# Loads one buffer further ahead, stores on ScalarE's queue, and half of the value scaling on ScalarE, in a fused mLSTM, MoE and MLP kernel

## The chip, the core and the metric

The kernel runs on one core of one Trainium2 chip. The metric is the device time of one execution in microseconds; three runs of the kernel before gave 841.56, 841.85 and 846.75 us, median 841.85.

## The reference, cut to what matters

Three stages in a row, all float32. Only the first, the recurrent attention, is touched by the change.

```
def _attn_ref(q, k, v, i_gate, f_gate, o_gate):      # 4 batches, 8 heads, 768 tokens, 40 dims
    for t in range(S):
        m_new = max(f_gate[t] + m, i_gate[t])
        f_stab = exp(f_gate[t] + m - m_new);  i_stab = exp(i_gate[t] - m_new)
        C = f_stab * C + i_stab * outer(v[t], k[t])   # 40 x 40 state of each head
        n = f_stab * n + i_stab * k[t]
        y[t] = sigmoid(o_gate[t]) * (C @ q[t]) / max(abs(n . q[t]), 1)
x = y as 3072 tokens x 320
x = _moe_ref(x)     # greedy routing of tokens to 8 experts, 384 each; relu(x @ w1) @ w2
return _moe2_ref(x) # elu(x @ w_in) @ w_out
```

## The kernel before, in words

**Chunks and units.** The 768 tokens are cut into 12 chunks of 64. A unit `u` is one chunk `n = u // 2` of one pair of batches `bp = u % 2`, both batches side by side on the 128 partitions, so there are 24 units. `Attention.run` (from L456) has one pass, here called step `u`, for each unit. Inside a chunk the recurrence is written as small matrix products: scores (q times k), values (the decayed scores P times the scaled values `vp`), recall (the faded query `qt` times the state C) and state (`kt` times `vp`, into `pC`). The steps are pipelined: step `u` runs the values, recall and state of unit `u`, the scores of unit `w = u + 2`, and prepares unit `v = u + 1`.

**What each engine does in a step, in the order of its queue.**
- TensorE (PE): values of `u` with scores of `w` (L368, L283), recall and state (L382, L394), three transposes of the rows `x` of unit `u - 1` (`turn`, L438), three logits matmuls on them (`logits`, L448), and the decay rows of `w` (`decay`, L291, into `pF` and `pD`).
- VectorE (DVE): the scan W and the weighted scores P of unit `v` (L309, L359), the reciprocal of the denominator `rd` (L414, L416, L418), the new state (L405), the rows `x` (L427).
- GpSimd (POOL): `vp` (all eight heads' values times the input gate, L316), `qt` (L319), the output gate `sg` (L420), `kt` (L328), the faded state C (L330).
- ScalarE (ACT): the copy `xT` of the transposes (L440), the sigmoid `sg` (L354), the logits copy `L` (L449), the copy `db` of the decays (L302), a copy inside `x` (L429).
- SyncE (SP): the DMA issues. At the end of step `u` it stores the two halves of `x` to DRAM (L432; the last two units' stores are on ScalarE's queue), and at the end of every even step it loads `qk` and `vk` of chunk `u // 2 + 2` (L254, L258).

Beside this, from step 4 on, ten pieces of the MLP's first weight, which arrive as 64-bit numbers, are loaded (`cx`, L856) and turned into float32 (DVE L873, L877, L880; ACT `cg` L868 and `wih` L926; POOL `wil` L928), and parts of the router run ahead (`early`, DVE L608 to L628). `fl` in `run` places these pieces at fixed points of the step by the tables FP and EP. Every engine executes its queue in the order in which the program issues it.

**Buffers.** `qk`, `vk` and `vp` have two buffers each. A load of chunk `n + 2` goes into the buffer of chunk `n`, which is last read by `qt` and `kt` of unit `2n + 1` in step `2n`. The chunk is first needed by the scores that run in step `2n + 2`.

After step 23 the router's rounds, the experts and the MLP follow, ordered by a planner with times of its own; the change does not touch them.

Of the kernel before, what the change touches and what calls it, by code (L numbers as in the profile page):

```python
# [8 lines left out]
F32 = mybir.dt.float32  # L9
# [3 lines left out]
AF = mybir.ActivationFunctionType  # L13
ALU = mybir.AluOpType
# [3 lines left out]
NS, NU = 12, 24  # L18
# [16 lines left out]
class Plan:  # L35
# [46 lines left out]
    def next(self):  # L82
        self.due(min(self.todo)[0])
# [30 lines left out]
class Attention:  # L114
# [4 lines left out]
    def __init__(self, nc, tc, consts, qk, vk, ig, fg, wg, xd, L, ident):  # L119
        self.nc, self.tc, self.qk, self.vk, self.xd, self.L, self.ident = nc, tc, qk, vk, xd, L, ident  # L120
        self.es = ExitStack()
        one = self.es.enter_context(tc.tile_pool(name="a1", bufs=1))
        self.two = self.es.enter_context(tc.tile_pool(name="a2", bufs=2))
        self.psX = self.es.enter_context(tc.tile_pool(name="psX", bufs=1, space=PS))
        V, G, A = nc.vector, nc.gpsimd, nc.scalar
# [16 lines left out]
        warm = one.tile([1, 8], F32, name="warm")  # L142
        V.memset(warm, 0.0)
        A.activation(warm, warm, AF.Exp)
        self.QKb = [one.tile([128, 2, 2, 8, 64], F32, name=f"qk{i}") for i in range(2)]
        self.QK, self.VK, self.W = {}, {}, {}
        for bp in range(2):
            self.load_qk(0, bp)
# [2 lines left out]
        self.wg = one.tile([128, 3, 8], F32, name="wg")  # L151
        nc.sync.dma_start(self.wg, wg)
        self.load_vk(1)
        self.VP = [one.tile([128, 8, 64], F32, name=f"vp{i}") for i in range(2)]
        m = one.tile([32, S + 1], F32, name="m")
        V.memset(m[:, 0:1], -1e30)
        d1 = one.tile([32, S], F32, name="d1")
# [92 lines left out]
        self.nc.scalar.activation(self.isT[:, n0:n1].rearrange("p n h -> p (n h)"), self.pG[:, n0 * 16:n1 * 16], AF.Copy)  # L250

    def load_qk(self, n, bp=slice(0, 2)):
        self.QK[n] = self.QKb[n % 2]
        self.nc.sync.dma_start(self.QK[n][:, bp], self.qk[n, :, bp])  # L254

    def load_vk(self, n):
        self.VK[n] = self.two.tile([128, 2, 968], F32, name="vk")
        self.nc.sync.dma_start(self.VK[n], self.vk[n])  # L258

    def by_token(self, u, i):  # L260
# [51 lines left out]
    def factors(self, u):  # L312
        G = self.nc.gpsimd
        n, bp = divmod(u, 2)
        i_ = self.isT[:, n, bp * 8:bp * 8 + 8, None].to_broadcast([128, 8, 41])
        G.tensor_tensor(self.VP[u % 2][:, :, :41], self.by_token(u, 0), i_, op=ALU.mult)  # L316
        if n > 0:
            qt = self.st["q", u] = self.two.tile([128, 8, 64], F32, name="qt")
            G.tensor_tensor(qt, self.QK[n][:, bp, 1], self.st["D", u], op=ALU.mult)  # L319
# [41 lines left out]
    def values(self, u):  # L361

        n, bp = divmod(u, 2)
        o = self.st["O", u] = self.psum("pO", 2)
        P = self.st.pop(("P", u))

        def one(h, r):
            self.nc.tensor.matmul(o[64 - r:128 - r, h], P[r:r + 64, h], self.VP[u % 2][r:r + 64, h], start=h == 0,  # L368
                                  stop=n == 0 and h == 7)

        return one
# [15 lines left out]
    def state(self, u):  # L387
        n, bp = divmod(u, 2)
        if n == NS - 1:
            return None  # L390
        kt = self.st.pop(("k", u))

        def one(h, r):
            self.nc.tensor.matmul(self.pC[r:r + 40, h], kt[r:r + 64, h], self.VP[u % 2][r:r + 64, h], start=True, stop=True)  # L394

        return one

# [24 lines left out]
    def rows_out(self, u):  # L422

        nc = self.nc
        n, bp = divmod(u, 2)
        x = self.st["x", u] = self.two.tile([128, 384], F32, name="x", bufs=3)
        nc.vector.tensor_tensor(x[:, :320].rearrange("p (h d) -> p h d", d=40), self.st.pop(("O", u))[:, :, :40],  # L427
                                self.st.pop(("sg", u)), op=ALU.mult)
        nc.scalar.activation(x[:, 320:], x[:, 256:320], AF.Copy)  # L429
        for r in range(2):  # L430
            row = (bp * 2 + 1 - r) * S + n * 64
            (nc.scalar if u > NU - 3 else nc.sync).dma_start(self.xd[row:row + 64], x[r * 64:r * 64 + 64])  # L432

    def turn(self, u):
        x = self.st.pop(("x", u))
# [20 lines left out]
    def run(self, hook, fill):  # L456
        later = self.later()
        for u in range(NU):
            v, w = u + 1, u + 2
            fl = lambda i: ([fill() for _ in range(FP[i])] if u > FU else []) + [self.step() for _ in range(EP[i])]  # L460
            self.both(self.values(u), self.scores(w))
            self.both(self.recall(u), self.state(u))
            if u > 0:
                self.turn(u - 1)
            if v < NU:
                self.scan(v)
                self.factors(v)
                self.opens(v)
                self.weigh(v)
            fl(0)  # L470
            if u < 3:
                next(later, None)
            self.gates(u, fl)
            if v < NU:
                self.fade(v)
            if u > 0:
                self.logits(u - 1)
            fl(2)
            if w < NU:
                self.decay(w)  # L480
            self.add_state(u)
            fl(3)
            if u == NU - 1:
                while self.extra:
                    self.step()
            self.rows_out(u)
            fl(4)
            if u % 2 == 0 and u // 2 + 2 < NS:
                self.load_qk(u // 2 + 2)
                self.load_vk(u // 2 + 2)  # L490
            if u == 0:
                self.turn_gi(2, NS)
                self.keep_gi(2, NS)
            hook(u)
        self.turn(u)
        self.logits(u)
        hook(NU)
        self.es.close()
# [1011 lines left out]
```

## Time and profile before

| | us |
|---|---|
| median of three runs | 841.85 |
| the profiled execution | 841.95 |
| its span, first to last instruction | 840.2 |
| attention, to the last stores of x | 0 to 187 |
| router, experts and MLP | 187 to 840 |

The profiled execution is 0.1 us from the median; 1.75 us of it lie outside the span. The profile is read by stage, because a mean over the whole span hides that attention is a chain of 24 short steps over five engines while the rest is one long run of matmuls.

### The profile page before, as it was taken

The numbers are of one execution on the slowest core, as the hardware profiler recorded it, in microseconds if no ns is written. First come the engines' busy times: TensorE is split into PE (matmuls) and PEld (weight loads), VectorE is DVE, ScalarE is ACT, GpSimd is POOL, SyncE is SP. The second block draws the span as 40 slices with busy tenths as digits, with TensorE's granted clock in tenths as the row PEclk, the third lists the DMA queues.
The fourth block names the chain that finished last, engine by engine and source line by source line (L and its number), as shares of the span: only waits on it lengthen the run. The fifth ranks groups of instructions, "written<-read, shape, count | busy, mean of one in ns | idle before, by whom it ended". The sixth has DMA issues, their size and how long they took to land.

```text
span 840.2 us, 18328 instructions
## 1 busy us (share of the span) xinstructions
PE 730.2 (87%) x7355; PEld 679.3 (81%) x7355; DVE 584.1 (70%) x1616; ACT 349.7 (42%) x743; POOL 309.7 (37%) x358
## 2 busy tenths in 40 slices
PE   7776667682889979989999999999999999999995
PEld 5665656571778878878988988899999999999995
DVE  8773776858788996688788778966942862662452
ACT  5322333333526652454354435424633643542431
POOL 3665776743622651352422414410601411211001
PEclk9765988895699989989999999999999999999998
DMA  5565565623520410220310301300310220100000
GB/s 206 182 245 169 164 261 174 221 54 110 181 63 19 149 64 25 84 83 1 128 62 3 112 17 63 104 24 2 128 40 24 91 76 25 63 1 25 1 1 24
DMA packets 20757, 72.79 MB, mean 87 GB/s; under 512 B 3200, under 2 KB 7296, under 8 KB 19264
## 3 DMA queue, kind: packets, MB, share of 16 engines
q1 hardware_dynamic: 11856, 39.41, 13.8%
q0 software_dynamic: 8448, 31.73, 11.4%
q8 instruction: 58, 0.95, 0.5%
q10 hardware_dynamic: 368, 0.49, 0.2%
q14 instruction: 27, 0.22, 0.1%
HBM read 62.96 MB, written 8.65 MB: 85 GB/s over the span
## 4 chain that ended last, share of the span: by engine, by line
PE 52%; DVE 16%; issue 6%; ACT 3%; DMA 0%; POOL 0%; POOLq 0%; ACTq 0%; DVEq 0%
PE ph L1096 24%; PE acc L1234 5%; PE acc L1238 4%; PE acc L1235 4%; PE acc L1203 3%; PE acc L1205 2%; PE acc L1204 2%; DVE e L1149 2%; PE pr L727 2%; DVE gl L980 1%; PE acc L1190 1%; DVE ge L713 1%; PE acc L1192 1%; PE ph L1049 1%; ACT e L1146 1%
## 5 line engine op out<-in xcount | busy, mean ns | idle before, releaser
L1234 PE MATMUL acc<-woh,gh 128*128 128x320 f32 x384 | 123.1, 321 | 0.0
L1238 PE MATMUL acc<-woh,gl 128*128 128x320 f32 x384 | 120.0, 312 | 0.0
L1235 PE MATMUL acc<-wol,gh 128*128 128x320 f32 x384 | 119.4, 311 | 0.0
L1149 DVE SCALAR_TENSOR_TENSOR e<-e,ph 128x384 f32<-128x384 f32 x128 | 69.8, 549 | 61.9 <-ACT e L1146 61.5
L1145 ACT ACTIVATE e<-ph 128x384 f32<-128x384 f32 x128 | 62.6, 489 | 117.4 <-PE ph L1096 113.0
L980 POOL TENSOR_TENSOR gl<-e,gh 128x384 fp32r<-128x384 f32 x33 | 34.4, 1045 | 165.2 <-DVE gh L974 129.9
L1096 PE MATMUL ph<-yh,wih 128*128 128x384 f32 x256 | 90.2, 352 | 0.4
L1096 PE MATMUL ph<-yh,wil 128*128 128x384 f32 x256 | 86.6, 338 | 0.0
L1113 ACT ACTIVATE gh<-ph 128x384 fp32r<-128x384 f32 x64 | 31.3, 491 | 123.0 <-PE ph L1096 121.8
L1244 POOL DMA_INDIRECT out_dram<-ot,idx x24 | 24.0, 998 | 141.3 <-ACT ot L972 138.0
L1120 DVE SCALAR_TENSOR_TENSOR gl<-ph,gh 128x384 fp32r<-128x384 f32 x64 | 35.3, 554 | 56.3 <-ACT gh L1113 55.9
L1238 PEld LDWEIGHTS acc<-woh,gl 128*128 128x128 f32 x384 | 72.8, 190 | 0.6
L1234 PEld LDWEIGHTS acc<-woh,gh 128*128 128x128 f32 x384 | 73.0, 190 | 0.2
L1235 PEld LDWEIGHTS acc<-wol,gh 128*128 128x128 f32 x384 | 73.0, 190 | 0.0
L1146 ACT ACTIVATE e<-e 128x384 f32<-128x384 f32 x128 | 67.3, 526 | 4.0
L1096 PE MATMUL ph<-yl,wih 128*128 128x384 f32 x256 | 66.8, 342 | 0.0
L283 PE MATMUL pS<-qk 64*64 64x64 f32 x768 | 37.5, 268 | 29.5 <-DMA qk<-in_qk_dram 29.5
L283 PEld LDWEIGHTS pS<-qk 64*64 64x64 f32 x768 | 33.5, 177 | 31.4 <-DMA qk<-in_qk_dram 31.4
L980 DVE TENSOR_TENSOR gl<-e,gh 128x384 fp32r<-128x384 f32 x95 | 57.3, 606 | 1.9
L1096 PEld LDWEIGHTS ph<-yh,wih 128*128 128x128 f32 x256 | 48.7, 190 | 4.5 <-ACT yh L1208 4.4
L1096 PEld LDWEIGHTS ph<-yh,wil 128*128 128x128 f32 x256 | 48.6, 190 | 0.0
L1096 PEld LDWEIGHTS ph<-yl,wih 128*128 128x128 f32 x256 | 46.6, 190 | 0.0
(269 smaller groups left out, 2033.2 us busy)
## 6 DMA issues: line engine op xcount, KB each, us to landing
vk<-in_vk_dram SPq DMA_DIRECT2D x12, 968.0 KB, 8.1
qk<-in_qk_dram SPq DMA_DIRECT2D x11, 1024.0 KB, 5.6
wx<-in_wout_dram SPq DMA_DIRECT2D x16, 320.0 KB, 2.8
xd<-x SPq DMA_DIRECT2D x44, 96.0 KB, 3.4
cx<-in_win_dram SPq DMA_DIRECT2D x8, 512.0 KB, 6.8
qk<-in_qk_dram SPq DMA_DIRECT2D x2, 512.0 KB, 5.4
cx<-in_win_dram SPq DMA_DIRECT2D x4, 256.0 KB, 6.2
xd<-x ACTq DMA_DIRECT2D x4, 96.0 KB, 2.2
```

The lines of the kernel that those rows point to most:

```text
L283: self.nc.tensor.matmul(p[r:r + 64, h], k, q, start=True, stop=True)
L980: (self.nc.vector if e == "d" else self.nc.gpsimd).tensor_tensor(out, x, y, op=ALU.subtract)
L1096: PE.matmul(p, w, x, start=k == 0, stop=k == 7)
L1113: nc.scalar.activation(h, p, AF.Relu)
L1120: nc.vector.scalar_tensor_tensor(l, p, 0.0, h, op0=ALU.max, op1=ALU.subtract)
L1145: nc.scalar.activation(e, p, AF.Relu, scale=-1.0)
L1146: nc.scalar.activation(e, e, AF.Exp, scale=-1.0)
L1149: nc.vector.scalar_tensor_tensor(e, e, -1.0, p, op0=ALU.add, op1=ALU.max)
L1203: PE.matmul(p, w[:, c], h, start=f == 0, stop=False)
L1234: PE.matmul(p, h[:, c], self.woh[:, f], start=f == 0, stop=False)
L1235: PE.matmul(p, h[:, c], self.wol[:, f], start=False, stop=False)
L1238: PE.matmul(p, l[:, c], self.woh[:, f], start=False, stop=f == 15)
```

## The change

Four edits, all in the attention stage. `qk`, `vk` and `vp` get a third buffer, and the loads of chunk `n + 2` move from the end of step `2n` to its start; they now go into the buffer of chunk `n - 1`. All stores of `x` go to ScalarE's queue. From unit 2 on, GpSimd scales four of the eight heads' values and ScalarE the other four, one instruction for each head. The logits matmuls of unit `u - 1` move behind the decay rows of unit `w`.

```
-        self.QKb = [one.tile([128, 2, 2, 8, 64], F32, name=f"qk{i}") for i in range(2)]
+        self.QKb = [one.tile([128, 2, 2, 8, 64], F32, name=f"qk{i}") for i in range(3)]
-        self.VP = [one.tile([128, 8, 64], F32, name=f"vp{i}") for i in range(2)]
+        self.VP = [one.tile([128, 8, 64], F32, name=f"vp{i}") for i in range(3)]
...
-        self.QK[n] = self.QKb[n % 2]
+        self.QK[n] = self.QKb[n % 3]
-        self.VK[n] = self.two.tile([128, 2, 968], F32, name="vk")
+        self.VK[n] = self.two.tile([128, 2, 968], F32, name="vk", bufs=3)
...
     def factors(self, u):
-        i_ = self.isT[:, n, bp * 8:bp * 8 + 8, None].to_broadcast([128, 8, 41])
-        G.tensor_tensor(self.VP[u % 2][:, :, :41], self.by_token(u, 0), i_, op=ALU.mult)
+        i_ = self.isT[:, n, bp * 8:bp * 8 + 8]
+        m = 8 if u < 2 else 4
+        G.tensor_tensor(self.VP[u % 3][:, :m, :41], self.by_token(u, 0)[:, :m], i_[:, :m, None].to_broadcast([128, m, 41]),
+                        op=ALU.mult)
+        for h in range(m, 8):
+            self.nc.scalar.activation(self.VP[u % 3][:, h, :41], self.by_token(u, 0)[:, h], AF.Copy, scale=i_[:, h:h + 1])
...
-            (nc.scalar if u > NU - 3 else nc.sync).dma_start(self.xd[row:row + 64], x[r * 64:r * 64 + 64])
+            nc.scalar.dma_start(self.xd[row:row + 64], x[r * 64:r * 64 + 64])
...
     def run(self, hook, fill):
+            if u % 2 == 0 and u // 2 + 2 < NS:
+                self.load_qk(u // 2 + 2)
+                self.load_vk(u // 2 + 2)
             self.both(self.values(u), self.scores(w))
...
-            if u > 0:
-                self.logits(u - 1)
             fl(2)
             if w < NU:
                 self.decay(w)
+            if u > 0:
+                self.logits(u - 1)
             self.add_state(u)
...
             fl(4)
-            if u % 2 == 0 and u // 2 + 2 < NS:
-                self.load_qk(u // 2 + 2)
-                self.load_vk(u // 2 + 2)
```

SyncE's queue before, in the middle of the attention stage (`qk_109` and `qk_110` are the two buffers, `xd<-x` the stores of the rows, `cx` pieces of the MLP's weight; `x4` is the stores of two steps):

```order
L432 DMA xd<-x 64x384 x2
L254 DMA qk_110<-in_qk_dram 128x2048
L258 DMA vk<-in_vk_dram 128x1936
L856 DMA cx<-in_win_dram 128x1024
L432 DMA xd<-x 64x384 x4
L856 DMA cx<-in_win_dram 128x1024
L254 DMA qk_109<-in_qk_dram 128x2048
```

The same queue in the changed kernel:

```order
L254 DMA qk_111<-in_qk_dram 128x2048
L258 DMA vk<-in_vk_dram 128x1936
L860 DMA cx<-in_win_dram 128x1024
L254 DMA qk_109<-in_qk_dram 128x2048
L258 DMA vk<-in_vk_dram 128x1936
L860 DMA cx<-in_win_dram 128x1024 x2
L254 DMA qk_110<-in_qk_dram 128x2048
```

Only loads are left in it, and three `qk` buffers take turns.

ScalarE's queue before, about one step of the attention stage:

```order
L440 ACTIVATE xT<-pX 128x384
L354 ACTIVATE sg<-vk 128x320
L449 ACTIVATE L<-pX 128x8
L302 ACTIVATE db<-pD 128x512
L868 ACTIVATE cg<-cx 128x512
L429 ACTIVATE x<-x 128x64
```

The same step in the changed kernel:

```order
L444 ACTIVATE xT<-pX 128x384
L320 ACTIVATE vp_121<-vk,isT 128x41 x4
L358 ACTIVATE sg<-vk 128x320
L302 ACTIVATE db<-pD 128x512
L453 ACTIVATE L<-pX 128x8
L872 ACTIVATE cg<-cx 128x512
L433 ACTIVATE x<-x 128x64
L436 DMA xd<-x 64x384 x2
```

Six entries a step are new, the four scaled heads behind `xT` and the two store issues behind the copy in `x`, and `db` now stands ahead of `L`.

## Rows read from the trace of the kernel before

**Rows 1.** Who waited for whom, 12 to 186 us: total us, times, longest.
```profile
ACT xT L440 <- PE pX L438: 77.8, 22, 7.9
POOL sg L420 <- DVE rd L418: 49.2, 17, 6.5
PE pS L283 <- DMA qk<-in_qk_dram: 29.5, 10, 5.0
```
**Rows 2.** SyncE's own waits, 12 to 186 us.
```profile
SPq L432 <- ACT x L429: 101.1, 20, 10.1
```
**Rows 3.** SyncE's timeline at the loads of step 8: start us, us, queue, line.
```profile
88.15 1.09 SPq L432 DMA_DIRECT2D xd<-x  x2
89.34 0.52 SPq L254 DMA_DIRECT2D qk<-in_qk_dram  x1
```
**Rows 4.** TensorE's timeline at the start of step 10.
```profile
94.43 0.37 PE L283 MATMUL pS<-qk 64*64 64x64 f32 x2 [2.93 <-DMA qk<-in_qk_dram]
```
**Rows 5.** Instructions on qk: duration ns min/median/max, first and last start us; landing.
```profile
L254 SPq DMA_DIRECT2D qk<-in_qk_dram x13: 367/526/1957, 1.2 to 161.5; - x13
...
DMA to landing us min/median/max: 4.4/5.6/10.2
```
**Rows 6.** Groups of instructions in steps 4 to 21: busy us, mean ns, idle before.
```profile
L302 ACT ACTIVATE db<-pD 128x512 f32<-128x512 f32 x18 | 10.8, 598 | 8.7 <-PE pD L291 6.9 <-POOL kt L328 1.3 <-POOL qt L319 0.5
L316 POOL TENSOR_TENSOR vp<-vk,isT 128x328 f32<-128x328 f32 x19 | 15.2, 800 | 0.0
L928 POOL TENSOR_TENSOR wil<-cF,wih 128x512 fp32r<-128x512 f32 x8 | 10.2, 1270 | 1.8 <-ACT wih L926 1.8
```
**Rows 7.** Stretch, us: busy PE, PEld, DVE, ACT, POOL, granted clock, DMA share, GB/s.
```profile
39.50:176.90 137.40, 93.67 (x2756) 83.55 (x2754) 94.65 (x199) 44.99 (x112) 93.17 (x101) 0.80 0.58 199
```
**Rows 8.** Waits of TensorE alone, steps 4 to 21 (39.5 to 176.9 us).
```profile
PE pS L283 <- DMA qk<-in_qk_dram: 27.6, 9, 5.0
PE pX L448 <- ACT xT L440: 10.4, 18, 0.6
```
**Rows 9.** Columns of rows 7 for step 7, most of step 21, 50 to 60 us.
```profile
68.60:75.10 6.50, 5.92 (x155) 5.32 (x153) 4.32 (x9) 2.33 (x6) 3.27 (x5) 0.61 0.52 134
172.40:177.00 4.60, 4.02 (x157) 3.62 (x156) 4.26 (x12) 1.78 (x5) 3.96 (x5) 1.00 0.19 46
50.00:60.00 10.00, 6.55 (x149) 5.53 (x142) 9.93 (x21) 3.49 (x9) 9.34 (x10) 0.66 0.59 209
```
**Rows 10.** ScalarE's timeline at the end of attention: the only stores on its queue.
```profile
181.42 1.34 ACTq L432 DMA_DIRECT2D xd<-x  x2
185.51 1.10 ACTq L432 DMA_DIRECT2D xd<-x  x2
```
**Rows 11.** Stores of x on SyncE, columns of rows 5.
```profile
L432 SPq DMA_DIRECT2D xd<-x x44: 445/549/1306, 20.9 to 178.4; - x44
```
**Rows 12.** ScalarE lines, columns of rows 5.
```profile
L429 ACT ACTIVATE x<-x x24: 238/252/258, 20.6 to 185.2; 128x64 f32<-128x64 f32 x24
L804 ACT ACTIVATE R<-kk,pc x8: 534/535/538, 210.9 to 594.8; 128x288 bf16<-128x288 bf16 x8
```
**Rows 13.** TensorE's timeline in step 21, without its 64x64 matmuls.
```profile
175.51 0.93 PE L448 MATMUL pX<-wg,xT 128*128 128x8 f32 x6 [0.58 <-ACT xT L440]
176.37 0.41 PE L291 MATMUL pF<-fp,sel 96*128 96x64 bf16 x8
```
**Rows 14.** GpSimd lines, columns of rows 5.
```profile
L316 POOL TENSOR_TENSOR vp<-vk,isT x24: 727/734/1365, 10.5 to 176.0; 128x328 f32<-128x328 f32 x24
L319 POOL TENSOR_TENSOR qt<-qk,db x22: 1256/1286/1461, 21.4 to 177.8; 128x512 f32<-128x512 f32 x22
L328 POOL TENSOR_TENSOR kt<-vk,W x22: 732/914/1318, 11.2 to 171.3; 128x320 f32<-128x320 f32 x22
L330 POOL TENSOR_TENSOR C<-C,db x20: 744/749/1200, 26.1 to 172.0; 128x328 f32<-128x328 f32 x20
L420 POOL TENSOR_TENSOR sg<-sg,rd x24: 712/722/862, 19.3 to 183.8; 128x320 f32<-128x320 f32 x24
```

More of the change, by code (lines that the diff above doesn't have):

```diff
@@ L367, in one @@
         def one(h, r):
-            self.nc.tensor.matmul(o[64 - r:128 - r, h], P[r:r + 64, h], self.VP[u % 2][r:r + 64, h], start=h == 0,
+            self.nc.tensor.matmul(o[64 - r:128 - r, h], P[r:r + 64, h], self.VP[u % 3][r:r + 64, h], start=h == 0,
                                   stop=n == 0 and h == 7)
@@ L393, in one @@
         def one(h, r):
-            self.nc.tensor.matmul(self.pC[r:r + 40, h], kt[r:r + 64, h], self.VP[u % 2][r:r + 64, h], start=True, stop=True)
+            self.nc.tensor.matmul(self.pC[r:r + 40, h], kt[r:r + 64, h], self.VP[u % 3][r:r + 64, h], start=True, stop=True)
         return one
```

## The prediction, made before the changed kernel was timed

> **What bounds the kernel now.** I read the waits first, then the busy times by stretch, then single steps and single lines. In the attention stage the waits [rows 1] name three things. TensorE stands idle 29.5 us for `qk` loads, 10 times. GpSimd waits 49.2 us for VectorE's reciprocal (which needs TensorE's recall), ScalarE 77.8 us for TensorE's transposes. The last two follow from the first: when TensorE stands at the scores of an even step, everyone behind it does too.
>
> The loads are late because of where they stand. SyncE executes in order and waited 101.1 us, in 20 waits, for ScalarE's copy inside `x` [rows 2]; the loads that the program puts at the end of step 8 were issued at 89.34, right behind two stores [rows 3], though step 9 was half over by then. TensorE came to the scores of step 10 at about 91.5 and stood 2.93 us, until 94.43 [rows 4]. A `qk` load lands 5.6 us after its issue at the median, 10.2 at most [rows 5]: one step is too short for it.
>
> Steps 4 to 21 (39.5 to 176.9 us) are the body: 18 steps (18 runs of `db`, [rows 6]) in 137.4 us [rows 7], so 7.63 us a step. TensorE waits in it 27.6 us for `qk` and 10.4 us (18 times 0.58) for `xT` ahead of the logits [rows 8]. Work per step, from the same row of [rows 7]: VectorE 94.65 / 18 = 5.26 us, GpSimd 93.17 / 18 = 5.18, ScalarE 44.99 / 18 = 2.50, DMA 0.58 x 137.4 / 18 = 4.43. TensorE works 4.02 us in a step of 4.6 at the full clock, 2.4 GHz [rows 9]. So no engine is full; the step is long because they wait for each other through the late load. Once it is early, the fullest engine decides.
>
> **The change, part by part.**
>
> *Loads earlier, third buffers.* The load of chunk n + 2 now waits for the readers of chunk n - 1, which finish in step 2n - 2 instead of 2n, and no store stands ahead of it on SyncE. That leaves about three steps until the scores need it, some 16 us at the step length found below, against 10.2 us for the slowest landing [rows 5]. On SyncE the loads still pass `cx` loads, which wait for VectorE to be done with an older `cx`. I cost that at nothing, because the three steps cover it; if not, rival D. The 27.6 us leave the body; what is late next is the step's busiest engine. The DMA's 4.43 us of work a step stay below that engine's, so the transfers fit.
>
> *Stores on ScalarE.* Two issues a step go to its queue. The only stores there so far took 1.34 and 1.10 us a pair [rows 10], mean 1.22. Bounds from the same stores on SyncE [rows 11]: 2 x 0.445 = 0.89 and 2 x 1.306 = 2.61. Queued behind them is `xT` of the next step, for which the logits on TensorE wait. What the edit brings is that SyncE no longer stands 101.1 us in front of stores that wait for ScalarE [rows 2]. The Trainium skill, "DMA: Bandwidth & Descriptors", section "Issuing engines are not separate DMA queues", speaks against this edit: DMAs started by different engines run on the same 16 DMA engines, and a second issuer only saves the first one's time for the issues. By it alone the edit would be worth SyncE's issue time, which nobody waits for, and the sum would hold only its cost on ScalarE; by [rows 2] the gain lies in the waits ahead of the issues, and I go by the rows.
>
> *Half of `vp` on ScalarE.* Four instructions of 41 elements for each unit. The nearest rows [rows 12]: 0.252 us for 64 elements with a constant scale, and 0.535 for 288 with a scale from a tile, as here. Bounds: 4 x 0.252 x 41 / 64 = 0.65 if time went with size alone, and 4 x 0.535 = 2.14. I take 0.30 each, near the 64-element row and a little above it for the scale from a tile: 1.2 us a step. GpSimd gives up half of 0.80 us [rows 6]: 0.40 at most, 0 if the cost were all fixed. I take 0.40, as these lines grow with size (0.8 us for 328 elements, 1.27 for 512). TensorE's heads 4 to 7 now wait for ScalarE, at a point half a microsecond into the next step, behind the logits that wait for the same queue's `xT` anyway.
>
> *Logits behind the decay rows.* In step 21 TensorE stands 0.58 us for `xT`, runs the logits from 175.51, then the decay [rows 13]. Now the decay, which starts at 176.37 and takes the half microsecond to the end of the step, fills that gap. TensorE's step falls from 4.6 to about 4.0 us. On VectorE nothing changes.
>
> *The new step.* VectorE 5.26, ScalarE 2.50 + 1.2 + 1.22 = 4.92, GpSimd 5.18 - 0.40 = 4.78, DMA 4.43, TensorE 4.02. VectorE is first, the next two close behind, so it won't be full: it was 9.93 of 10 us busy from 50 to 60 us [rows 9], its best, and 69% over the body [rows 7]. With both neighbours above 90% of its load I take 92%, nearer to the best: 5.26 / 0.92 = 5.72 us, 18 x 5.72 = 102.9 us, 34.5 us less than 137.4.
>
> Outside the body: one `qk` wait is left, 29.5 - 27.6 = 1.9 us in step 2, and goes: 2. The last two steps need no load and lose the gap of 0.58 us twice; their stores were on ScalarE before: 1. The first steps get the stores and one more memset on GpSimd, under the start-up's waits: 0. What follows attention is the same work on the same data and moves up whole.
>
> **Sum:** 34.5 + 2 + 1 = 37.5; 841.95 - 37.5 = 804.5, rounded 805. The profiled execution is 0.1 us from the median, so this stands for both.
>
> **The rivals.**
>
> *A, the forecast:* a VectorE-bound step, from 797 (VectorE 99% full, 5.30 us a step) to 811 (86% full, 6.1 us). For it: most waits in [rows 1] hang on TensorE, and steps that need no load already run in 4.6 us.
>
> *B, a neighbour becomes the bound.* GpSimd's lines run from 0.73 to 1.32 us (`kt`), from 0.74 to 1.20 (C), up to 1.46 (`qt`) [rows 14]. If a fuller VectorE drives each to its maximum, with half of `vp`'s 1.365: 0.68 + 1.46 + 1.32 + 1.20 + 0.86 + 10.2 / 18 for `wil` = 6.09 us; 18 steps are 109.6, the total 811. The Trainium skill, "SBUF — State Buffer", section "SBUF: two separate sides", describes such a thing: GpSimd and a VectorE instruction with two SBUF inputs take turns on one port pair, whoever comes second waits the whole instruction. That the rows split into two lengths agrees. Or ScalarE at 2.50 + 2.14 + 1.34 = 5.98 us gives 809. Against it: the medians of four of the five GpSimd lines lie next to the minimum.
>
> *C, the clock.* With TensorE working 4 of 5.7 us its clock may fall more often. Step 7 ran at a granted clock of 0.61, mostly on the lower level, 1.2 GHz, with TensorE busy 5.92 us, and took 6.5 us [rows 9]. All 18 steps at that: 117 us, total 819. Against it: step 21 has gaps too, TensorE busy 4.02 of 4.6 us, and kept 1.00 [rows 9].
>
> *D, the loads come no earlier,* because a `cx` load that waits for its buffer holds the `qk` load behind it on SyncE. The 27.6 us stay, only the gaps of 0.58 us go: 10.4 + 1.2, total 830. For it: SyncE is in order and carries both. Against: three steps of room.
>
> *E, slower.* The place is ScalarE's queue. Some issues take far longer than the median: a `qk` issue took 1.96 us [rows 5]. If the stores on ScalarE meet the same behind a fuller DMA, the step is 2.50 + 2.14 + 2 x 1.96 = 8.56 us, longer than 7.63; 18 steps add 16.7 us, total 859. It decides once stores and scaled heads exceed 7.63 - 2.50 = 5.13 us a step. Against: the four stores there took 1.22 a pair.
>
> **How the numbers follow.** A 0.60, B 0.15, C 0.10, D 0.07, all faster by over 1% (8.4 us, about what a measurement of this kernel can tell from no change). E 0.04; the same mechanism just at 5.13 us, no change, 0.04. So faster 0.92, same 0.04, slower 0.04. The range takes in A, B and C, 0.85 of the chance: from 795, two below A's end for the phases of the clock in what follows, to 820. The time is A's, 805.
>
> **What would show it.** Right: TensorE's waits for `qk` near 0; steps of 5.3 to 6.1 us; VectorE above 86% busy in the body; attention's last store near 150 us; ScalarE's four copies near 1.2 us and a pair of issues near 1.2 us. Wrong: waits for `qk` left (D); ScalarE without gaps while VectorE waits (B or E); GpSimd lines at their maxima (B); a granted clock well under 0.80 in the body (C). A saving in attention that later stages give back would break the assumption that the rest moves up whole.

## The result, and the profile after

The changed kernel took 821.65 us at the median of four runs (815.46 to 828.93), the kernel before 844.30 beside it on the same chip. The ratio is 0.9706, 95% interval 0.9626 to 0.9786: some 25 us faster, where the sum had 37.5. The profiled execution below is the slowest of the four (828.93 us at a mean granted clock of 0.912; the others had 0.920 to 0.936); it counts as a slow run and the ratio leaves it out, while the profiles of two kernels that differ from this one in one part each (loads_late and stores_sp, in the table below) are of fast runs and show nearly the same body.

Two stretches in the columns of [rows 7]: the body (steps 4 to 21), then what follows step 21.

```profile
44.40:163.60 119.20, 98.12 (x2756) 90.96 (x2756) 91.14 (x190) 57.46 (x185) 86.85 (x98) 0.73 0.56 188
163.60:827.20 663.60, 607.39 (x3923) 571.90 (x3922) 458.87 (x1359) 286.92 (x596) 195.62 (x209) 0.96 0.18 58
```

The body is 119.2 us instead of 137.4, 6.62 us a step where 5.72 were forecast. What follows takes 663.6 us (663.3 before), so it moved up whole. The start lost: step 4 begins at 44.4 us instead of 39.5. In sum 4.9 - 18.2 + 0.3 = -13.0, which is 841.95 to 828.93. The last store of `x` starts at 172.7 us; the forecast had it near 150.

TensorE's waits in the body, against [rows 8]:

```profile
PE pC L398 <- issue: 5.5, 2, 2.8
PE pO L386 <- issue: 3.7, 3, 2.5
PE pC L398 <- POOL kt L332: 3.1, 5, 1.5
PE pS L283 <- issue: 2.9, 1, 2.9
PE pD L291 <- issue: 1.2, 1, 1.2
PE pX L452 <- ACT xT L444: 1.2, 4, 0.6
```

The 27.6 us for `qk` are gone altogether, the 10.4 us for `xT` are 1.2. In their place stands "issue", time in which the engine waited for nothing that the profile can name: 13.1 us in six waits of over 0.3 us (3.4 us in two before). They come at four different lines, so no single tile is late.

The engines' parts: the scaled heads, the stores, and the landing of a `qk` load (mean ns stands behind the busy time in the first two lines; min/median/max in the others). The four copies of a step overlap, so their busy time is less than 72 times the mean.

```profile
L320 ACT ACTIVATE vp<-vk,isT 128x41 f32<-128x41 f32 x72 | 17.6, 319 | 0.0
L317 POOL TENSOR_TENSOR vp<-vk,isT 128x164 f32<-128x164 f32 x19 | 13.1, 687 | 0.0
L317 POOL TENSOR_TENSOR vp<-vk,isT x24: 453/640/1371, 10.8 to 162.5; 128x164 f32<-128x164 f32 x22, 128x328 f32<-128x328 f32 x2
L436 ACTq DMA_DIRECT2D xd<-x x48: 452/572/1324, 21.3 to 172.7; - x48
DMA to landing us min/median/max: 4.6/7.6/13.8
```

SyncE's waits from 12 to 186 us; in [rows 2] it waited 101.1 us for the stores' `x`:

```profile
SPq L860 <- DVE cF L881: 57.4, 8, 14.0
SPq L860 <- DMA xd<-x: 27.6, 1, 27.6
SPq L254 <- POOL qt L323: 13.3, 4, 5.7
```

Now `cx` loads stand at its head, and the `qk` loads behind them.

**What "issue" is.** One of the six waits, on TensorE's timeline, with the DMA queues in the 2.7 us ahead of it and in half a microsecond within it (packets, MB, share of the 16 DMA engines; the last stretch is 99.7 to 100.2 us):

```profile
99.21 0.22 PE L398 MATMUL pC<-vp,kt 64*40 64x64 f32 x1
102.21 0.33 PE L398 MATMUL pC<-vp,kt 64*40 64x64 f32 x2 [2.79 <-issue]
...
q1 hardware_dynamic: 116, 0.85, 87.6%
q10 hardware_dynamic: 39, 0.06, 5.9%
...
q1 hardware_dynamic: 18, 0.12, 58.8%
q10 hardware_dynamic: 32, 0.04, 19.7%
q8 instruction: 1, 0.02, 12.2%
```

0.4 us into the wait one packet of the queue `q8`, kind "instruction", starts (at 99.82); 2.4 us later TensorE goes on. The whole run has 58 such packets:

```profile
q8 instruction: 58, 0.95, 0.5%
```

That is 16.4 KB each, and the trace has 14,812 records of TensorE, 255 for one packet. The waits lie where that says. These rows run from one wait's end to a later one's; the counts behind PE and PEld are the recorded matmuls and weight loads.

```profile
61.57:70.42 8.85, 6.31 (x126) 5.96 (x127) 4.59 (x10) 2.93 (x10) 5.23 (x6) 0.50 0.84 289
70.42:102.20 31.78, 24.80 (x761) 22.81 (x760) 26.86 (x52) 16.46 (x52) 25.79 (x28) 0.82 0.65 221
102.20:140.59 38.39, 31.51 (x887) 28.78 (x888) 29.15 (x63) 19.53 (x62) 29.28 (x33) 0.77 0.67 226
```

253, 1521 and 1775 instructions: 1, 6 and 7 times 253 or 254 (256 with the records of TensorE's sequencer). So TensorE's instructions come in blocks of 256, by DMA, in a queue that the profile counts on the same 16 engines as the loads. Counted in the trace, a packet starts when the block before the one it brings begins to run: after attention, where DMA has little to do, within 44 records of that point in every run here. If it is late by a whole block, TensorE stands. From 14 to 190 us the fourteen kernels of this document have 90 "issue" waits of over 0.3 us on TensorE; counted in the traces, 85 of them end 2.2 to 2.6 us after the start of such a packet and the other five 2.7 to 3.1, though a packet comes only every 5 us or so. The wait at 61.58 us is at the same instruction as one of the two that the kernel before had in its body:

```profile
64.30 0.44 PE L394 MATMUL pC<-vp,kt 64*40 64x64 f32 x4 [1.95 <-issue]
```

By the Trainium skill, "Runtime: NRT & Kernel Launch", section "Instruction fetch mechanics", instructions are refilled in 16 KiB blocks of 256 while the current block runs, and crossing a block is mostly hidden. The trace agrees on the size (16.4 KB a packet). Mostly hidden agrees for the kernel before (3.4 us in two waits of 137.4 us of body); in the changed kernel six of the body's about 22 blocks were not hidden, for 13.1 us.

**What it costs beside the wait.** The wait of 3.77 us in step 2, what follows it, and a step at the full clock:

```profile
27.00:30.85 3.85, 0.08 (x7) 0.01 (x1) 3.44 (x4) 0.87 (x4) 1.64 (x2) 0.88 0.87 281
30.85:37.80 6.95, 4.34 (x52) 3.75 (x52) 1.92 (x7) 3.68 (x9) 4.80 (x18) 0.50 0.69 256
37.80:44.40 6.60, 6.60 (x154) 6.38 (x153) 4.41 (x14) 2.37 (x9) 4.08 (x9) 0.50 0.24 72
44.40:51.00 6.60, 6.60 (x154) 6.35 (x154) 3.31 (x8) 2.47 (x10) 3.34 (x6) 0.50 0.14 32
79.90:84.10 4.20, 4.09 (x154) 3.65 (x154) 3.83 (x5) 3.02 (x11) 3.80 (x5) 1.00 0.33 71
```

Behind the wait the clock is at its lower level, 1.2 GHz, and stays there through steps 3 and 4, in which TensorE has not one gap: it takes 6.60 us for what takes 4.20 at 2.4 GHz. So TensorE, which I had as the least loaded engine of the new step (4.02 us), bounds such steps. The body's clock is 0.73.

### The profile page after: what moved, and what is told of

Same layout as the page of the kernel before. It is cut to its first block, busy times and chain, and to the rows that moved or that the text cites. A ratio compares the mean times of both kernels' runs of the same rounds, so it can differ in the third digit from the quotient of the medians.

```text
span 827.2 us, 18408 instructions
## 1 busy us (share of the span) xinstructions
PE 738.1 (89%) x7355; PEld 690.2 (83%) x7355; DVE 583.3 (71%) x1616; ACT 365.4 (44%) x831; POOL 304.8 (37%) x359
## 4 chain that ended last, share of the span: by engine, by line
PE 62%; DVE 20%; issue 10%; ACT 5%; POOL 2%; DMA 1%; ACTq 1%; POOLq 0%; DVEq 0%
PE ph L1100 24%; PE acc L1238 5%; PE acc L1242 4%; PE acc L1239 4%; PE acc L1207 3%; PE acc L1209 3%; PE acc L1208 3%; PE pO L372 2%; DVE e L1153 2%; PE pX L452 2%; PE pO L386 2%; PE pr L731 2%; DVE gl L984 1%; PE acc L1194 1%; DVE ge L717 1%
## 5 line engine op out<-in xcount | busy, mean ns | idle before, releaser
L398 PE MATMUL pC<-vp,kt 64*40 64x64 f32 x704 | 36.0, 272 | 12.7 <-issue 9.3
L1100 PE MATMUL ph<-xh,w1h 128*128 128x384 f32 x128 | 45.0, 351 | 0.3 <-DVE gl L1124 0.2
```

The source lines that it names most:

```text
L1100: PE.matmul(p, w, x, start=k == 0, stop=k == 7)
```

## Experiments

**Theories.** F: the blocks of instructions come late behind the loads' transfers; TensorE stands, its clock falls, and the saved `qk` wait is partly paid back there. C: the clock falls by itself, since TensorE works only part of each step. Q: ScalarE's longer queue sets the step. Twelve kernels; ratios are to the kernel before on the same chip, with 95% intervals. Issue waits are those over 0.3 us. Body, waits and clock are of one profiled execution of each kernel, the ratio of several runs, so small differences between bodies say little: 110.7 us (vp_gpsimd) and 118.1 us (stores_logits) go with the same ratio within the intervals.

| kernel | ratio | body us | qk wait | issue wait | clock in body |
|---|---|---|---|---|---|
| before | 1 | 137.4 | 27.6 | 3.4 | 0.80 |
| changed | 0.9706 [0.9626, 0.9786] | 119.2 | 0 | 13.1 | 0.73 |
| no_late_loads | 0.9560 [0.9522, 0.9598] | 103.8 | 0 | 1.7 | 0.85 |
| loads_late | 0.9701 [0.9655, 0.9746] | 116.7 | 0 | 11.9 | 0.75 |
| stores_sp | 0.9702 [0.9664, 0.9740] | 115.4 | 0 | 16.7 | 0.82 |
| half_loads | 0.9717 [0.9673, 0.9762] | 117.7 | 0 | 17.2 | 0.78 |
| before_no_late | 0.9700 [0.9656, 0.9745] | 111.2 | 0 | 0.9 | 0.86 |
| loads_by_scalar | 0.9750 [0.9708, 0.9792] | 115.9 | 0 | 11.9 | 0.81 |
| before_stores_scalar | 0.9677 [0.9635, 0.9719] | 113.8 | 0.3 | 4.9 | 0.79 |
| vp_gpsimd | 0.9684 [0.9647, 0.9721] | 110.7 | 0 | 8.3 | 0.78 |
| stores_logits | 0.9661 [0.9593, 0.9730] | 118.1 | 0 | 13.7 | 0.68 |
| loads_only | 0.9725 [0.9637, 0.9812] | 119.4 | 0 | 5.5 | 0.79 |
| vp_logits_only | 0.9963 [0.9932, 0.9995] | 136.0 | 37.4 | 1.4 | 0.77 |
| half_bytes | 0.9671 [0.9591, 0.9751] | 112.3 | 0 | 10.5 | 0.80 |

**no_late_loads.**

```
             if u % 2 == 0 and u // 2 + 2 < NS:
-                self.load_qk(u // 2 + 2)
-                self.load_vk(u // 2 + 2)
+                n = u // 2 + 2
+                if n < 3:
+                    self.load_qk(n)
+                    self.load_vk(n)
+                else:
+                    self.QK[n], self.VK[n] = self.QK[n - 3], self.VK[n - 3]
```

> Changed kernel with the qk and vk loads of chunks 3 to 11 left out (chunks 3 to 11 compute on the data of chunks 0 to 2). All other work stays. Theory F (TensorE's instruction blocks come late behind a deep queue of loads, it stands 2.5 to 3.8 us each time, and its clock falls after that): without these loads the idle times of TensorE that end in 'issue' fall from 17 us in the first 164 us to under 4, the granted clock of the body rises from 0.73 to 0.9 or more, the 18 body steps take 100 to 106 us instead of 119, the total is 800 to 808 us. Theory C (the clock falls by itself because a step of 5.5 us leaves TensorE a quarter idle): the idle times go, the clock stays under 0.8 and the body above 112 us, total 812 to 820. Theory Q (ScalarE's longer queue, 4.9 us of work a step, sets the step): nothing moves, 818 to 824.

Measured 811.39 us (808.76 to 813.18), 38 us under the kernel before on this chip, and 5.77 us a step. The body's row and what is left of the waits:

```profile
40.50:144.30 103.80, 87.33 (x2755) 79.72 (x2754) 92.36 (x188) 57.98 (x185) 86.69 (x98) 0.85 0.29 78
...
PE pC L398 <- POOL kt L332: 6.9, 8, 2.1
PE pF L291 <- DVE W L309: 2.5, 5, 0.6
PE pX L452 <- ACT xT L444: 1.9, 4, 0.7
PE pO L386 <- issue: 1.7, 2, 1.1
```

The same instructions on all engines, without the traffic: the issue waits go, the clock rises to 0.85, and VectorE is 92.36 / 103.8 = 89% busy. This is about the step I had forecast (5.72). F had a clock of 0.9 or more and 800 to 808 us; the clock stayed under that, and the time came out 3 us over, on a chip on which the kernel before took 849.53. C and Q fall for the bulk: TensorE has the same matmuls and ScalarE the same queue. But 0.85 still means that about 31 of the 104 us ran at 1.2 GHz (0.15 / 0.5 of them; by the same sum 64 of 119 in the changed kernel), so a good part of the low clock has little to do with late blocks. The kernel by itself does not tell the blocks from other things that traffic may slow. The busy times speak against these: VectorE, GpSimd and ScalarE took 92.36, 86.69 and 57.98 us here and 91.14, 86.85 and 57.46 us with the traffic; only TensorE's waits and its busy time, which goes with its clock, moved.

**loads_late**, **stores_sp**, **half_loads** on the changed kernel:

```
loads_late:  loads at the end of the even step again, two buffers for qk and vk
-            nc.scalar.dma_start(self.xd[row:row + 64], ...)          # stores_sp
+            (nc.scalar if u > NU - 3 else nc.sync).dma_start(self.xd[row:row + 64], ...)
-            if u % 2 == 0 and u // 2 + 2 < NS:                       # half_loads
-                self.load_qk(u // 2 + 2)
-                self.load_vk(u // 2 + 2)
+            n = u // 2 + 2
+            if n < NS:
+                self.load_qk(n, u % 2)
+                self.load_vk(n, u % 2)
```

> Changed kernel with the loads put back to the end of the even step and two buffers for qk and vk; stores on ScalarE, split values, third vp buffer and late logits stay. All theories: if the gain is from the early loads, TensorE waits for qk again; without stores ahead of the loads on SyncE these waits may be shorter than the 29.5 us of the kernel before, I expect 15 to 25 us, and 828 to 838 us. If the total is below 822 the early loads were worth nothing and the gain came from the other three parts.

> Changed kernel with the stores back on SyncE's queue (all else stays). There they stand ahead of the loads again and pace them: a load is issued at its own step, not as soon as a buffer is free. Theory F: the queue of loads is shallower, the idle times of TensorE on 'issue' fall below 8 us, waits for qk stay under 5 us thanks to the third buffer, total 805 to 815. Theory Q: ScalarE loses 1.2 us a step, the body gets shorter by up to 10 us with the idle times on 'issue' unchanged, total 808 to 815. Theory C: no change, 816 to 824.

> Changed kernel with each chunk's loads cut in two, one half at the start of each step instead of both at the start of the even one. Same bytes. Theory F: loads come in smaller heaps, the idle times on 'issue' fall to about half (8 us) and the total to 808 to 815. Theories C and Q: no change, 816 to 824.

Undoing the early loads or the stores' new queue changes nothing: 823.40 and 822.65 us, no wait for `qk` in either. Either of the two edits makes the loads early enough, and the second adds nothing; loads_late came out faster than I had it. Half a chunk for each step (826.92 us) gains nothing over the changed kernel either; it has the longest issue wait of all, 5.4 us:

```profile
PE pO L387 <- issue: 8.0, 3, 5.4
```

In stores_sp and half_loads F missed. It expected issue waits of under 8 and of about 8 us, and 805 to 815 and 808 to 815 us; they came to 16.7 and 17.2 us, and the ratios stayed at that of the changed kernel (0.9702 and 0.9717 against 0.9706), as C had it. So pacing or cutting the loads does not bring the blocks earlier. Q misses in stores_sp too, where ScalarE gave up the stores and nothing was won. And stores_sp, with more issue waits than the changed kernel, has the higher clock (0.82): the clock does not follow the sum of these waits.

**before_stores_scalar**, **loads_only**, **vp_logits_only**: parts of the change alone.

```
-            (nc.scalar if u > NU - 3 else nc.sync).dma_start(...)    # before_stores_scalar
+            nc.scalar.dma_start(...)
loads_only:      third buffers of qk and vk, loads ahead of the step; nothing else
vp_logits_only:  third vp buffers, four heads' values on ScalarE, logits behind the decay; nothing else
```

> The kernel before with one part of the change alone: all stores of x are issued by ScalarE; loads stay at the end of every second step with two buffers, vp stays on GpSimd, the logits stay ahead of the decay. Theory F: SyncE no longer holds the loads behind the stores, the waits for qk fall from 27.6 us to under 8, and the waits ended by 'issue' rise from 3.4 to 8-15 us; time 0.968-0.980 of before, most of the whole change's gain. Rival D (the loads are held by the cx loads and by their late place in the program, not by the stores): qk waits stay over 18 us and the time is 0.985-1.00 of before.

> The kernel before with the early loads alone: third buffers for qk and vk, loads ahead of the step. Stores stay on SyncE, vp on GpSimd, logits ahead of the decay. Theory F: two steps of lead are enough although stores and cx loads stand ahead on SyncE; waits for qk under 2 us, issue 5-15 us, xT about 10 us as before, time 0.966-0.976, as with the stores alone (0.968): the two are one remedy done twice. Rival D (the stores hold the loads on SyncE for as long as they are led): qk waits over 10 us, 0.980-0.990.

> The kernel before with the other two parts alone: values of four heads scaled by ScalarE (third vp buffers), logits behind the decay. Loads and stores stay as before. Theory F: the loads still land when the stores let them, so the time taken from xT (10.4 us) comes back as a longer wait for qk (27.6 us to 32-40); body 134-139 us, time 0.993-1.003. Rival L (each wait is a term of its own): xT goes, qk stays at 27.6, body 125-128 us, 0.985-0.989.

The stores alone give 816.15 us, the early loads alone 827.78, the two others alone 846.56 (all of the gain; about all of it, with an interval that reaches 0.9812; next to nothing). TensorE's waits in the bodies of before_stores_scalar (first three lines), loads_only (next three) and vp_logits_only:

```profile
PE pX L448 <- ACT xT L440: 12.5, 18, 1.3
PE pO L382 <- issue: 1.9, 1, 1.9
PE pS L283 <- DMA qk<-in_qk_dram: 0.3, 1, 0.3
```
```profile
PE pX L448 <- ACT xT L440: 10.4, 18, 0.6
PE pC L394 <- POOL kt L328: 8.6, 8, 3.1
PE pO L368 <- issue: 2.5, 3, 1.4
```
```profile
PE pS L283 <- DMA qk<-in_qk_dram: 37.4, 9, 6.8
PE pC L398 <- POOL kt L332: 2.1, 1, 2.1
```

In the last, the 10.4 us for `xT` are gone and the nine `qk` waits are 9.8 us longer: TensorE comes earlier to a load that lands when it did. Issue waits stay small there, as F says: while TensorE stands for `qk`, its next block arrives. The issue waits came out under the range expected in before_stores_scalar and near its low end in loads_only.

**stores_logits.**

```
before_stores_scalar, and in run():
-            if u > 0:
-                self.logits(u - 1)
             fl(2)
             if w < NU:
                 self.decay(w)
+            if u > 0:
+                self.logits(u - 1)
```

> The kernel before with two parts of the change: the stores issued by ScalarE, and the logits behind the decay. Loads stay late with two buffers, vp stays on GpSimd. With the stores alone TensorE waited 12.5 us for xT and 4.9 us with 'issue' in the body of 113.7 us. Theory F (a block of 256 instructions is asked for when the one before it starts; a wait taken out of a block only leaves the next block less time to arrive): xT goes under 2 us, the issue waits rise to 9-14 us, the body stays within 3 us of 113.7, time 0.963-0.972 of before. Rival L (each wait taken from TensorE is time won): body 102-106 us, 0.954-0.960.

822.12 us, ratio 0.9661, the same as with the stores alone within the intervals; the body is 4.3 us longer than there, where F allowed 3 (the profiled run, 825.27 us, is the longest of its four). Its row and waits:

```profile
38.30:156.40 118.10, 101.89 (x2755) 96.14 (x2754) 92.08 (x197) 43.72 (x112) 92.88 (x101) 0.68 0.65 214
...
PE pO L368 <- issue: 3.8, 2, 2.6
PE pC L394 <- issue: 3.4, 2, 2.7
PE pO L382 <- issue: 2.7, 2, 1.9
PE pD L291 <- issue: 2.1, 1, 2.1
PE pS L283 <- issue: 1.3, 1, 1.3
PE pX L448 <- ACT xT L440: 1.2, 1, 1.2
```

This sets F apart from L most sharply. Nothing was added to any queue and no byte to the traffic; 11.3 us of waits for `xT` were taken from TensorE, 8.8 us came back as waits with "issue", and PE's busy time grew from 93.88 to 101.89 us, as the clock fell from 0.79 to 0.68. Rival L (a wait taken is time won) fails: it had a body of 102 to 106 us and a ratio of 0.954 to 0.960, which only the low end of the interval reaches.

**vp_gpsimd**: `m = 8 if u < 2 else 4` becomes `m = 8`.

> The changed kernel with all eight heads' values scaled by GpSimd again; early loads, stores on ScalarE and late logits stay. Theory F: GpSimd is not what sets the step in the body, so 0.965-0.976 of before, the same as the changed kernel (0.971) within 0.6%. Rival B (GpSimd sets the step): GpSimd is busy 0.1 to 0.4 us longer a step and loses the four small instructions of ScalarE as cover, the waits of TensorE for kt grow from 2.9 us to 6-10 and the time goes to 0.978-0.985.

816.78 us, ratio 0.9684: the four instructions on ScalarE are worth nothing here. TensorE's waits for `kt` grew to 5.9 us, near rival B's, but the time did not follow.

**before_no_late**: the edit of no_late_loads on the kernel before, from the buffers of two chunks earlier.

> The kernel before, with the loads of qk and vk for chunks 3 to 11 left out (the buffers of two chunks earlier are read again); everything else stays as before. Theory F (blocks of TensorE's instructions come late behind the loads; what the change won on qk it paid there): the 27.6 us of waits for qk go, the waits that end with 'issue' stay at 0 to 3 us, since no backlog of loads is left for the blocks to wait behind; the body goes from 137.4 to 106-111 us and the time to 0.960-0.968 of before, within 1% of the run in which the changed kernel lost the same loads (0.956). Rival S (the new places of stores, logits and vp carry a large part of the gain by themselves): the body stays at 118 us or more, 0.975 of before or above, because the 10.4 us of waits for xT and new waits behind GpSimd take the place of qk.

818.34 us, ratio 0.9700, above F's range and below the rival's. The body is 111.2 us; issue waits are 0.9 us, but the 10.4 us for `xT` stay and TensorE waits 13.1 us for `kt`:

```profile
PE pC L394 <- POOL kt L328: 13.1, 9, 4.8
PE pX L448 <- ACT xT L440: 10.4, 18, 0.6
```

So the other parts of the change do bring something, 0.9700 against 0.9560 in another set of runs, once the loads are out of the way; by these waits it is probably the new places of `vp` and logits, but no run separates them from the stores' queue here. With the loads running it is not to be seen.

**loads_by_scalar**, **half_bytes**: attempts to shorten what a block waits behind.

```
loads_by_scalar, per step: half a chunk's qk by ScalarE at its start, half of vk by ScalarE ahead of the decay; stores on SyncE
+            if n < NS: self.load_qk(n, u % 2, self.nc.scalar)
...
+            if n < NS: self.load_vk(n, u % 2, self.nc.scalar)
half_bytes:
+                bp = slice(0, 2) if n < 3 else 0
+                self.load_qk(n, bp)
+                self.load_vk(n, bp)
```

> The changed kernel with the loads of qk and vk taken off SyncE's queue, where they are let go in bunches behind the cx loads: half a chunk's qk is issued by ScalarE at the start of every step, half a chunk's vk by ScalarE in the middle of it (after the gates); the stores go back to SyncE. All bytes are loaded as before. Theory F: the backlog that a block of instructions meets shrinks from some 2.5 MB to about 0.5 to 1 MB, the waits ended by 'issue' fall from 13.1 us in the body to under 6, the body goes from 119.2 to 106-112 us and the time to 0.957-0.964 of before. Theory C (the clock falls by itself) and theory Q (ScalarE's queue sets the step): the body stays at 115-120 us, 0.970-0.975 of before, with or without the issue waits.

> The changed kernel with half the bytes of the late loads: for chunks 3 to 11 only the first half of each chunk's qk and vk is loaded (the odd steps read what lies in the buffer), by as many issues in the same places. Theory F: the waits with 'issue' go with the bytes that stand ahead of a block; between 13.1 us (all bytes) and 1.7 us (none) they come to 4-9 us, the body to 107-113 us and the time to 0.960-0.967 of before. Rival N (the number of issues and the place of the loads on SyncE matter, not the bytes): issue waits 11-17 us, 0.968-0.974 as for the changed kernel.

Both miss what F expected. Smaller transfers, let go at even distances, made the longest issue wait shorter (2.4 us) but left their sum at 11.9 us and the time at 821.52 us, where C and Q had it. Half the bytes gave 10.5 us of issue waits, between the two ranges, and 823.12 us (0.9671, at F's upper edge). Counted in the trace, a block's packet starts in the mean 0.8 and 1.0 us after its point without the late loads, 1.75 us with half of them, 1.8 to 2.3 us with all, in bunches or spread (1.4 us in the two kernels in which TensorE still stands for `qk`). So F holds for the traffic as a whole; what of it a packet waits behind is open.

None of the twelve beats the changed kernel beyond its interval with all the work done; one edit of the four, the stores on ScalarE, does as well.

## Why the prediction was right and wrong

**Sign and first step: right.** What bound the kernel was the `qk` load held behind stores on SyncE [rows 2 to 4]. Moving the stores alone gives 0.9677. By the Trainium skill's rule that issuers share the same DMA engines ("DMA: Bandwidth & Descriptors", section "Issuing engines are not separate DMA queues") this edit would have saved only the time of the issues; but SyncE's queue also held whatever stood behind a waiting store (101.1 us, [rows 2]), and that was the gain. I counted early loads and moved stores as one remedy of two parts; each is the whole remedy by itself.

**Loads ahead of `qk` on SyncE cost nothing: right.** They do hold it (57.4 us at `cx`, rival D's mechanism), and a load lands in 7.6 us instead of 5.6 [rows 5], 13.8 at most, but three steps cover that: no wait for `qk`.

**Costs on ScalarE: right.** 0.319 us a head against 0.30, 0.98 us of busy time a step against 1.2, 2 x 0.572 = 1.14 us for a pair of stores against 1.22. ScalarE was busy 48% of the body. **GpSimd's saving: too large.** The mean of 0.80 us [rows 6] became 0.687, a saving of 0.11 instead of 0.40. The shortest runs went from 727 [rows 14] to 453 ns, 0.27 us less; but 12 of the 22 half-size runs took about 640 or 910 ns, and those eat most of it. What makes them longer, no run isolates.

**Logits behind the decay: the mechanism right, its worth wrong.** The gap closed (10.4 to 1.2 us), a step at the full clock fell to 4.2 us. But it turned into issue waits (stores_logits) or a longer `qk` wait (vp_logits_only).

**The new step: wrong, and here the 13 us went** (the profiled body lost 18.2 us of the 34.5 forecast). The step that failed is the sentence "The DMA's 4.43 us of work a step stay below that engine's, so the transfers fit." Their bytes fit; but TensorE's own instructions ride on the same engines, and a block that is late by more than one block's run stops it. Once `qk` no longer made TensorE stand, it ran into that: 13.1 us of waits and 98.12 us of busy time at clock 0.73, against 1.7 and 87.33 us at 0.85 without the late loads. The sum had TensorE at 4.02 us a step, its time at the full clock, and put the lower level at nothing; it worked 98.12 / 18 = 5.45 us. VectorE was 91.14 / 119.2 = 76% busy, not 92%. The 5.26 / 0.92 = 5.72 us is near what a body without the late loads' traffic took (5.77).

**Outside the body:** what follows moved up whole, as assumed. In the profiled run the first steps cost 4.9 us instead of giving 2; the 3.77 us with "issue" in step 2 and the low clock behind it are most of that. The other kernels with all their loads reached step 4 between 37.8 and 43.1 us, so the loss of 4.9 us is of this execution, and whether the 2 us were won can't be told.

**Rivals.** C, at 0.10, came nearest: 6.5 us a step and 819 us against 6.62 and 821.65, its mark (a clock well under 0.80) is there. But its cause, that TensorE works only part of a step, fails as the whole cause on no_late_loads (0.85). Nor are the late blocks the whole cause: 0.85 is not 1, and stores_sp has more of these waits at 0.82. That C's number fits is in part luck. The row for the late blocks was before me: two "issue" waits of 1.95 and 1.45 us in the body before, with TensorE's blocks in the list of DMA queues. B did not happen: GpSimd was busy 86.85 / 119.2 = 73% of the body. E did not happen: no issue of a store took over 1.324 us; once `xT` stood 4.5 us for a store that had not landed. The median lies 1.65 us over the range's end; the ratio times the 841.85 us of before gives 817.1, inside it.

**Open:** whether the small differences among the kernels with all loads (0.966 to 0.975, intervals mostly overlapping) are real; what exactly a block's packet waits behind; and how much of the lower clock is the issue waits' doing: both are least without the late loads, but among the kernels with all loads they do not go together.

## What to carry to other kernels

A wait that you remove may have been hiding another one that runs on the same resource; ask what else the waiting engine was being served with while it stood. In a stretch of many small matmuls under heavy loads, a block of 256 instructions lasted only 5 to 6 us here (31.78 / 6 and 38.39 / 7), so look for the waits ended by "issue" and for the queue of kind "instruction" before you forecast that an engine will be full. When several edits attack one wait, time each alone: here one line of four edits carried the gain.

## What the runs showed of the hardware that was not expected

- TensorE stood up to 5.4 us (half_loads) for a block of its own instructions; 16.4 KB a packet, at most one block ahead, resumed 2.2 to 2.6 us after the packet's start in 85 of 90 waits (stores_sp: packet at 88.33, on again at 90.58 after 4.48 us; the changed kernel: 99.82 and 102.21).
- TensorE's clock stayed at 1.2 GHz for two whole steps, 37.8 to 51.0 us, in which it had no gap, before it rose again.
- Halving the elements of GpSimd's product took its shortest run from 727 to 453 ns, but its mean from 800 to 687 ns only; ScalarE's 41-column product took 319 ns, and four of them 0.98 us a step.
